# Four moves in the order of work of a two-layer linear-attention and MLP kernel

## The chip, the cores and the metric

The kernel runs on one core of one Trainium2 chip, in one launch. The metric is the device time of that core in microseconds, from several runs of the same program. Engine names are those of the profile: PE is TensorE's matmul (PEld its weight load), DVE is VectorE, ACT is ScalarE, POOL is GpSimd, SP is SyncE, which here issues all DMAs.

## The reference

Two layers, each an attention part A and an MLP part B with residuals, on x of 2048 rows by 640 columns in float32. Layernorm has no weights.

```python
x = x + A(layernorm(x)); x = x + B(layernorm(x))      # twice, same weights

def A(x):                       # 32 heads of 20 columns
    q, k, v = split(x @ wqkv)
    pq, pk = q @ w_phi, k @ w_phi                      # per head, 20 x 20
    phi_q = concat(softmax(pq), softmax(-pq))          # 40 features
    phi_k = concat(softmax(pk), softmax(-pk))
    kv, z = phi_k^T v, sum_s phi_k                     # sums over all rows
    return ((phi_q kv) / (phi_q z + 1e-6)) @ wo

def B(x):                       # 640 -> 1536 -> 640
    h = x @ w1 + b1
    return (h * tanh(softplus(h))) @ w2
```

## The kernel before, in words

Every large product is made of three matmuls of float32r parts: each operand is split into a high part (a copy on ACT, `fold_high`, `Transposed.high`, L376, L290) and a low part (a subtraction, `fold_low` L294, `Transposed.lower` L384, `make_parts` L172), and `project_half` (L446, matmul at L451) multiplies high by high, high by low and low by high. The rows are taken in 8 blocks of 256, each of two tiles of 128.

*Layer by layer.* For each layer `attend_first` (L501) makes features of keys and queries, stores the queries' features transposed to DRAM (`e_d`, L564) and sums phi_k^T v over all rows into one PSUM tile, `kva` (matmuls at L546; the profile has 128 records for two tiles, 2048 in all). `attend_second` (L815) loads the queries' features again (`load`, L769, DMAs at L778 and L796), multiplies by the finished sums (`average`, L825, matmuls at L839), divides, transposes and multiplies by wo (`Rows.half`, L866). `dense` (L949) is the MLP: matmuls at L963 and L1014.

*Blocks of `attend_first`.* The loop at L685 takes for every block the six projections in `order`: in blocks 2 to 6 `k0 k1 v0 v1 q0 q1` (tile 0 and tile 1 of keys, values, queries). Each is a generator. `next(g)` starts one (its matmuls and the copy out of PSUM); `advance()` (L524) gives every pending generator, newest first, one further step. In `features` (L462) the steps are: subtract the per-head maximum and minimum (L477 to L480, one subtraction on POOL or DVE), one exponential on ACT (L483), the sums and their reciprocal and the scaling (L488 to L491; the scaling mostly on POOL). A yield between two of them puts the next step one projection later. `held(i)` (L515) says how many further projections a key tile waits before its sums at L546. The first step, L467, is a POOL memset of the query or key tile. Query tiles have two buffers, so the third query tile (block 1, tile 0) uses that of the first, whose four stores (L564) must have landed.

*The next block's rows.* While block b is projected, block b+1 is prepared: at n = 0 its x is loaded and its mean and variance are computed on DVE and POOL (`fetch_normed`, L504), at n = 2 the rows are normalized on ACT (`normed`, L401, activation at L409), and at n = 3, 4, 5 `nxt.step()` transposes them on PE (L367) and splits them. In layer two the rows come normalized and transposed from DRAM (`load_turned`, L425) and are only split, their low parts on POOL.

*What sets the order.* The kernel is written in one block whose instructions a planner orders by a simulated timeline: on each engine it takes, of the instructions that are ready in its simulation, the one written first. Three things bind it. `act` (L129) ties every activation that goes through it behind the one written before; in the profile all of these have its line, L135. `tc.issue_after(x)` ties instructions behind `x` where both are on one engine. In `written()` (L121, the start of layer one) and in `attend_second` from L877 (PE and SP alone) the order is the written one. On the chip every engine runs its instructions in the order that was planned.

*Blocks of `attend_second`.* L903: an odd block first averages the next two blocks of queries (four groups, 44 records each in the profile), then the two tiles of the block are multiplied by wo in halves, each added to x (L869). SP gets, in written order: the x of block b+1 (L914; its buffer must have been stored), in odd blocks the features of blocks b+3 and b+4 (`phi`, L899), at the end of each block the store of the new x (L937), and then `fetches[b + 1]()` (L940): the raw rows of the MLP weights (L164; 768 KB for a row block of w1, two or three loads of 320 KB for w2) that `makes[b + 1]()` (L938) splits on ACT and POOL at the end of the block after. `fetches[0]` stands ahead of the loop (L888).

*Value tiles.* `v_halves(apart)` (L142) gives one tile of the tag `v` (two buffers) or, with `apart`, two half tiles of the tag `ol` (six buffers), each filled by activations of its own. A value tile and the key tile's features (`big`, five buffers) live until the sums at L546 have read them.

Of the kernel before, what the change touches and what calls it, by code (L numbers as in the profile page):

```python
# [44 lines left out]
def kernel(  # L45
# [416 lines left out]
    def features(ps, e, pool_sub, scale=nc.gpsimd, late=False, after_low=False):  # L462
# [22 lines left out]
        if late:  # L485
            yield
# [14 lines left out]
    def attend_first(layer, x_src, first):  # L501
# [13 lines left out]
        def held(i):  # L515

            b, t = divmod(i, BT)
            if layer and b == 1:
                return (3, 2)[t]
            if not layer and b < 2:  # L520
                return ((3, 1), (4, 1))[b][t]
            return int(t == 0 and b < NB - 1)
# [8 lines left out]
        def keys(xts, i, v):  # L531
            e = big_tile()
            yield from features(project(xts, i % BT, kv_ws, 0, w=QC), e, False,
                                nc.vector if i == NT - 1 else nc.gpsimd, layer and i // BT == 1,
                                not layer and i // BT == 1)
            yield
            for _ in range(held(i)):
                yield
            opens = not summed[0]
            summed[0] = True  # L540
            for r in range(9):
                for j in range(4):
                    h = 3 * (4 * (r // 3) + j) + r % 3
                    if h < H:
                        c, g = divmod(h, H // 2)
                        nc.tensor.matmul(kva[32 * j:32 * j + DH + 1, 40 * r:40 * r + 40],  # L546
                                         v[1][c][:, (DH + 1) * g:(DH + 1) * (g + 1)], e[:, 40 * h:40 * h + 40],
                                         start=(opens and r == 0), stop=(i == NT - 1), skip_group_check=True)

        def queries(xts, i, ps=None):  # L550
            e = query_tile(i)
            yield from features(project(xts, i % BT, q_ws, 0, w=QC) if ps is None else ps, e, not layer or i != BT,
# [132 lines left out]
        for b in range(NB):  # L685
# [10 lines left out]
            vs = [v_halves(b == 2 or (b == 0 and not layer)) for _ in range(BT)]  # L696
# [4 lines left out]
            for n, (kind, t) in enumerate(order):  # L701
# [6 lines left out]
                if b == 0 and n == (1 if layer else 3):  # L708
                    kva = one_tile()
                    nc.vector.memset(kva[:, :360], 0.0)  # L710
# [4 lines left out]
                if b + 1 < NB:  # L715
                    if n == 0 and (b or layer):
                        xt = fetch_normed(b + 1)
                    elif n == 2:
# [15 lines left out]
                else:  # L734
                    next(g)
                    if layer and b == 0 and n == 0:
                        turn()
                    advance()
# [76 lines left out]
    def attend_second(x_src, x_dst, acc, fetches, makes, fetch_next, begin_next):  # L815
# [61 lines left out]
        with tc.manual_schedule(engines={mybir.EngineType.PE, mybir.EngineType.SP}):  # L877
# [25 lines left out]
            for b in range(NB):  # L903
# [11 lines left out]
                if b % 2:  # L915
                    phi(b + 3)
# [22 lines left out]
                if b + 1 < NB:  # L939
# [248 lines left out]
```

## Time and profile before

| what | before |
|---|---|
| median of 3 runs | 1351.21 us (1350.4 to 1353.28) |
| the profiled execution's own time | 1352.93 us |
| its span, first to last instruction | 1351.1 us |
| granted TensorE clock, mean | 1.000 |
| PE busy | 99%, 13056 matmuls |
| DVE, ACT, POOL busy | 77%, 43%, 36% |
| DMA | 174.24 MB, mean 129 GB/s over the span |
| layer one: `attend_first`, `attend_second`, `dense` | to about 245, 351 and 685 us |
| layer two: the same | to about 905, 1010 us and the end |

The profile is of one execution. PE's busy time says that matmuls were in flight, not that they followed one another as closely as they can: their ends are modelled, so the steps between their starts are to be read beside it. A wait names the instruction or transfer whose semaphore came last; "issue" is a wait that nothing in the profile ends. The time of the profiled execution is 1.8 us more than its span.

### The profile page before, as it was taken

The numbers are of one execution on the slowest core, as the hardware profiler recorded it, in microseconds if no ns is written. First come the engines' busy times: TensorE is split into PE (matmuls) and PEld (weight loads), VectorE is DVE, ScalarE is ACT, GpSimd is POOL, SyncE is SP. The second block draws the span as 40 slices with busy tenths as digits, with TensorE's granted clock in tenths as the row PEclk, the third lists the DMA queues.
The fourth block names the chain that finished last, engine by engine and source line by source line (L and its number), as shares of the span: only waits on it lengthen the run. The fifth ranks groups of instructions, "written<-read, shape, count | busy, mean of one in ns | idle before, by whom it ended". The sixth has DMA issues, their size and how long they took to land.

```text
span 1351.1 us, 31372 instructions
## 1 busy us (share of the span) xinstructions
PE 1343.4 (99%) x13056; PEld 1334.2 (99%) x13056; DVE 1043.1 (77%) x1741; ACT 575.3 (43%) x978; POOL 484.1 (36%) x479
## 2 busy tenths in 40 slices
PE   9999999999999999999999999999999999999998
PEld 9999999999999999999999999999999999999998
DVE  6698898876687877778769788789759776677775
ACT  5343444222454554445443334332236444444443
POOL 3266654334322222222226655634351211111112
PEclk9999999999999999999999999999999999999999
DMA  9545445698714442234474544548974231233200
GB/s 329 174 102 121 98 99 108 169 286 271 216 29 91 118 118 72 61 104 114 122 239 109 124 90 90 98 99 255 291 253 117 79 75 37 85 98 98 78 21 21
DMA packets 353359, 174.24 MB, mean 129 GB/s; under 512 B 288193, under 2 KB 324785, under 8 KB 353217
## 3 DMA queue, kind: packets, MB, share of 16 engines
q1 hardware_dynamic: 353217, 172.25, 47.2%
q8 instruction: 102, 1.67, 0.5%
q14 instruction: 40, 0.33, 0.1%
HBM read 106.34 MB, written 65.86 MB: 127 GB/s over the span
## 4 chain that ended last, share of the span: by engine, by line
PE 93%; DVE 3%; DMA 2%; SPq 1%; POOL 1%; issue 1%; ACT 0%; POOLq 0%; ACTq 0%; DVEq 0%
PE one L963 25%; PE mm L1014 24%; PE mm L451 24%; PE one L451 12%; PE mm L839 3%; PE one L367 2%; PE one L546 2%; PE one L1014 1%; DVE r L488 1%; DVE m L477 1%; DMA e_d<-r 1%; PE one L839 1%; DMA xt<-in_x 1%; DMA wp_d<-r1l 1%; SPq L564 0%
## 5 line engine op out<-in xcount | busy, mean ns | idle before, releaser
L989 POOL TENSOR_TENSOR ol<-big,ol 128x512 fp32r<-128x512 f32 (+1 forms) x98 | 132.0, 1347 | 471.5 <-ACT ol L988 401.8
L1014 PE MATMUL mm<-r2h,ol 128*128 128x320 f32 x1240 | 295.8, 309 | 0.0
L963 PE MATMUL one<-xtl,r1h 128*128 128x256 f32 x960 | 268.4, 280 | 0.0
L963 PE MATMUL one<-xth,r1l 128*128 128x256 f32 x960 | 268.2, 279 | 0.0
L963 PE MATMUL one<-xth,r1h 128*128 128x256 f32 x960 | 266.1, 280 | 0.0
L1014 PEld LDWEIGHTS mm<-r2h,ol 128*128 128x128 f32 x1240 | 212.1, 188 | 0.0
L1014 PE MATMUL mm<-r2l,ol 128*128 128x320 f32 x620 | 190.9, 309 | 0.0
L451 PE MATMUL mm<-r1h,xth 128*128 128x304 f32 (+1 forms) x600 | 184.7, 308 | 0.0
L451 PE MATMUL mm<-r1h,xtl 128*128 128x304 f32 (+1 forms) x600 | 183.9, 307 | 0.3 <-POOL xtl L384 0.3
L451 PE MATMUL mm<-r1l,xth 128*128 128x304 f32 (+1 forms) x600 | 184.0, 307 | 0.0
L963 PEld LDWEIGHTS one<-xth,r1l 128*128 128x128 f32 x960 | 180.5, 188 | 0.0
L963 PEld LDWEIGHTS one<-xtl,r1h 128*128 128x128 f32 x960 | 180.4, 188 | 0.0
L963 PEld LDWEIGHTS one<-xth,r1h 128*128 128x128 f32 x960 | 179.8, 188 | 0.0
L978 DVE TENSOR_SCALAR big<-big 128x512 f32<-128x512 f32 (+1 forms) x98 | 55.6, 567 | 120.7 <-ACT big L976 116.3
L976 ACT ACTIVATE big<-one,b1s 128x256 f32<-128x256 f32 x192 | 81.0, 468 | 102.5 <-PE one L963 102.2
L491 POOL TENSOR_TENSOR r<-r,r 128x1280 f32<-128x1280 f32 x32 | 77.8, 2432 | 115.9 <-DVE r L489 105.7
L988 ACT ACTIVATE ol<-big 128x512 fp32r<-128x512 f32 (+1 forms) x98 | 60.7, 620 | 136.3 <-DVE big L987 136.2
L1014 PEld LDWEIGHTS mm<-r2l,ol 128*128 128x128 f32 x620 | 116.5, 188 | 0.0
L980 ACT ACTIVATE big<-big,two 128x512 f32<-128x512 f32 (+1 forms) x98 | 70.1, 715 | 105.6 <-DVE big L979 105.5
L451 PEld LDWEIGHTS mm<-r1h,xth 128*128 128x128 f32 x600 | 112.8, 188 | 0.8
L451 PEld LDWEIGHTS mm<-r1h,xtl 128*128 128x128 f32 x600 | 112.9, 188 | 0.5 <-POOL xtl L384 0.5
L451 PEld LDWEIGHTS mm<-r1l,xth 128*128 128x128 f32 x600 | 112.8, 188 | 0.1
(179 smaller groups left out, 3136.8 us busy)
## 6 DMA issues: line engine op xcount, KB each, us to landing
e_d<-r SPq DMA_DIRECT2D x128, 160.0 KB, 4.0
big<-e_d SPq DMA_DIRECT2D x30, 640.0 KB, 7.7
x_d<-xt SPq DMA_DIRECT2D x23, 640.0 KB, 5.9
xt<-x_d SPq DMA_DIRECT2D x22, 640.0 KB, 4.2
n_d<-xn SPq DMA_DIRECT2D x168, 80.0 KB, 2.2
xt<-in_x SPq DMA_DIRECT2D x16, 640.0 KB, 4.6
xn<-x_d SPq DMA_DIRECT2D x28, 320.0 KB, 4.5
v<-n_d SPq DMA_DIRECT2D x30, 256.0 KB, 3.1
```

Of the source, the lines that this page charges most:

```text
L367: nc.tensor.transpose(ps[:, c, t * P:(t + 1) * P], self.rows[t][:, (c0 + c) * P:(c0 + c + 1) * P], ident)
L451: last_product[0] = nc.tensor.matmul(ps[:, :w], a[:, sl], r, start=(k == 0 and n == 0), stop=(k == KD - 1 and n == 2)).ins
L491: ins = scale.tensor_tensor(eg, eg, r.unsqueeze(2).to_broadcast([P, 2 * H, DH]), op=ALU.mult).ins
L546: nc.tensor.matmul(kva[32 * j:32 * j + DH + 1, 40 * r:40 * r + 40], v[1][c][:, (DH + 1) * g:(DH + 1) * (g + 1)], e[:, 40 * h:40 * h + 40], ...
L839: nc.tensor.matmul(po[c][64 * q:64 * q + 64, GW * j:GW * j + w], phs[g][:n, s0:s0 + 64], kvb[:n, g, :w], start=True, stop=True)
L963: nc.tensor.matmul(ph[:, j, :], l, r, start=(n == 0), stop=(n == 3 * KD - 1))
L976: exps[0] = nc.scalar.activation(part(ta, 0)[:, j - js.start], ph[:, j, :], AF.Exp, bias=b1s[:, 2 * pr + j:2 * pr + j + 1]).ins
L978: nc.vector.tensor_scalar_min(e, e, E_CAP)
L980: nc.scalar.activation(r, n, AF.Ln, bias=two)
L988: nc.scalar.activation(ah[:, js], n, AF.Copy)
L989: nc.gpsimd.tensor_tensor(al[:, js], n, ah[:, js].bitcast(F32), op=ALU.subtract)
L1014: ins = nc.tensor.matmul(pys[t][c][:, :HC], (ah, ah, al)[n][:, j, t * P:(t + 1) * P], w, start=(f == 0 and n == 0), stop=(f == KF - 1 and ...
```

## The change

- `features`: `late` becomes a number of extra yields ahead of the sums. The first query tile of layer one (`i == 0`) gets one, so that its sum, reciprocal, scaling and transpose stand one projection later; in `b == 0` this is behind `last_fold[0]`, the low parts of the folded key weights. In layer two the two key tiles of block 1 get 2 and 1 instead of 1 and 1.
- `held`: in layer one, blocks 2 to 5, key tiles are held 3 and 2 projections instead of 1 and 0, so both tiles' sums stand after the next block's third projection (its first value tile) instead of after its first. In layer two, block 1, both are held 2 instead of 3 and 2.
- `v_halves`: in layer one, blocks 0, 2, 4 and 6 take half tiles, instead of 0 and 2.
- `kva`'s memset in layer one stands behind the last low part of the folded weights on DVE.
- Block 2's rows (layer one, while block 1 is projected) are normalized after the start of the second projection and ahead of its `advance()`, instead of ahead of the third.
- `attend_second`: the raw weights for odd blocks are loaded within their own block, behind the averages and the load of the next x and ahead of `phi`, instead of at the end of the block before. Those for even blocks stay.

```diff
--- before.py
+++ after.py
@@ -459,7 +459,7 @@
     def query_tile(i):
         return r2_wide(10 + i % 2, F32).rearrange("p s d -> p (s d)")
 
-    def features(ps, e, pool_sub, scale=nc.gpsimd, late=False, after_low=False):
+    def features(ps, e, pool_sub, scale=nc.gpsimd, late=0, after_low=False):
 
         eg = e.rearrange("p (g d) -> p g d", d=DH)
         eh = e.rearrange("p (h s d) -> p s h d", s=2, d=DH)
@@ -482,7 +482,7 @@
         yield
         act(e, e, AF.Exp)
         yield
-        if late:
+        for _ in range(late):
             yield
         r = work.tile([P, 2 * H], F32, tag="r", name="r", bufs=2)
         nc.vector.tensor_reduce(r, eg, axis=AX.X, op=ALU.add)
@@ -516,9 +516,11 @@
 
             b, t = divmod(i, BT)
             if layer and b == 1:
-                return (3, 2)[t]
+                return 2
             if not layer and b < 2:
                 return ((3, 1), (4, 1))[b][t]
+            if not layer and b < NB - 2:
+                return (3, 2)[t]
             return int(t == 0 and b < NB - 1)
 
         def advance():
@@ -531,7 +533,7 @@
         def keys(xts, i, v):
             e = big_tile()
             yield from features(project(xts, i % BT, kv_ws, 0, w=QC), e, False,
-                                nc.vector if i == NT - 1 else nc.gpsimd, layer and i // BT == 1,
+                                nc.vector if i == NT - 1 else nc.gpsimd, (BT + 2 - i) * (layer and i // BT == 1),
                                 not layer and i // BT == 1)
             yield
             for _ in range(held(i)):
@@ -549,7 +551,7 @@
 
         def queries(xts, i, ps=None):
             e = query_tile(i)
-            yield from features(project(xts, i % BT, q_ws, 0, w=QC) if ps is None else ps, e, not layer or i != BT,
+            yield from features(project(xts, i % BT, q_ws, 0, w=QC) if ps is None else ps, e, not layer or i != BT, late=int(not layer and not i),
                                 after_low=not layer and i // BT == 1)
 
             b, t = divmod(i, BT)
@@ -693,7 +695,7 @@
                 order = ("v0", "k0", "q0", "v1", "k1", "q1")
             elif b == NB - 1:
                 order = ("k0", "k1", "v0", "v1", "q0")
-            vs = [v_halves(b == 2 or (b == 0 and not layer)) for _ in range(BT)]
+            vs = [v_halves(b == 2 or (not layer and b % 2 == 0)) for _ in range(BT)]
             if 2 <= b < 2 + KD and not layer:
                 with tc.issue_after(last_act[0]):
                     o_ws.append(next(o_gen))
@@ -707,7 +709,8 @@
                         advance()
                 if b == 0 and n == (1 if layer else 3):
                     kva = one_tile()
-                    nc.vector.memset(kva[:, :360], 0.0)
+                    with (nullcontext() if layer else tc.issue_after(last_fold[0])):
+                        nc.vector.memset(kva[:, :360], 0.0)
                 if b == NB - 1 and n == 3:
                     loaded = {0: load(0)}
                     loaded[1] = load_groups(1, 0) + load_rest(1)
@@ -715,7 +718,7 @@
                 if b + 1 < NB:
                     if n == 0 and (b or layer):
                         xt = fetch_normed(b + 1)
-                    elif n == 2:
+                    elif n == 2 and (layer or b != 1):
                         nxt = xt if layer else normed(b + 1, xt, not b)
                     elif n > 2:
                         nxt.step()
@@ -735,6 +738,8 @@
                     next(g)
                     if layer and b == 0 and n == 0:
                         turn()
+                    if b == 1 and n == 1 and not layer:
+                        nxt = normed(2, xt)
                     advance()
                 pending.append(g)
             if b == 1:
@@ -913,6 +918,7 @@
                 if 0 < b < NB - 1:
                     xs[b + 1] = fetch(x_src, b + 1)
                 if b % 2:
+                    fetches[b]()
                     phi(b + 3)
                     phi(b + 4)
                 if b == NB - 3:
@@ -936,7 +942,7 @@
                 xt = xs.pop(b)
                 nc.sync.dma_start(row_block(x_dst, b), xt)
                 makes[b]()
-                if b + 1 < NB:
+                if b % 2 and b + 1 < NB:
                     fetches[b + 1]()
                 tail()
                 if b < NB - 1:
```

## The prediction

> **What bounds the kernel now.** I read the page first: the span, the busy time of each engine, and the chain that ended last.
>
> ```profile
> span 1351.1 us, 31372 instructions
> ...
> PE 1343.4 (99%) x13056; PEld 1334.2 (99%) x13056; DVE 1043.1 (77%) x1741; ACT 575.3 (43%) x978; POOL 484.1 (36%) x479
> ...
> PE 93%; DVE 3%; DMA 2%; SPq 1%; POOL 1%; issue 1%; ACT 0%; POOLq 0%; ACTq 0%; DVEq 0%
> ```
>
> TensorE (PE) is busy for 1343.4 of 1351.1 us, and the change takes no matmul away. Only the time in which PE stands still, or changes from one kind of matmul to another, can be won. So the next view is the list of PE's waits, which is whole here.
>
> ```profile
> PE one L451 <- issue: 1.6, 1, 1.6
> PE one L92 <- POOL ident masks.py:199: 1.3, 1, 1.3
> PE one L367 <- ACT xn L135: 1.0, 1, 1.0
> PE mm L451 <- POOL xtl L384: 0.3, 1, 0.3
> ```
>
> Of the four waits the second is the start and stays. The other three are one place each, and each lies where the change works. These idle times count from a modelled end of the matmul before; what the end can win is the step between starts, which I read from PE's timeline. The most that the change can win is thus a few microseconds, a fifth to a third of a percent.
>
> **Part 1: rows of block 2, and the first query's sum.** PE's timeline, columns start and duration:
>
> ```profile
> 60.32 0.31 PE L451 MATMUL mm<-r1h,xth 128*128 128x320 f32 x1
> 60.47 0.31 PE L451 MATMUL mm<-r1l,xth 128*128 128x320 f32 x1
> 61.80 0.33 PE L367 MATMUL one<-ident,xn 128*128 128x128 f32 x1 [1.02 <-ACT xn L135]
> ```
>
> The second step is 1.33 us, where matmuls of this shape start 0.15 apart: 1.2 us lost, on the transposes of block 2's normalized rows. The chain of waits says what came before:
>
> ```profile
> 52.77 1.20 POOL r L478
> ...
> 54.82 0.19 DVE mv L342 x2
> ```
>
> ACT and POOL in the same stretch, from their timelines:
>
> ```profile
> 56.40 1.13 POOL L352 TENSOR_SCALAR stats<-mv,stats 128x1 f32<-128x1 f32 x2
> 59.67 1.27 ACT L135 ACTIVATE big<-big 128x1280 f32<-128x1280 f32 x1 [2.97 <-DVE big L480]
> 60.84 1.72 ACT L135 ACTIVATE xn<-xt,stats 128x640 f32<-128x640 f32 x2
> ```
>
> The statistics are there at 57.53 (56.40 + 1.13), yet the two normalizations run at 60.84, because every activation of this stretch is held in the order in which it is written, and an exponential that waits for DVE until 59.67 stands ahead. The change writes the normalizations ahead of that step's `advance()`, so ahead of this exponential. They could then run from 57.55 to 59.27 (1.72 for both), in ACT's idle 2.97 us, and the exponential still starts at 59.67: nothing is pushed. The tiles are ready 1.2 us before PE now asks for them at 60.6. If PE is given the transposes at once, before the next projection, it comes at about 59.0 (eleven steps of 0.15 earlier) and waits 0.3. I take 1.2 won; bounds 0.9 and 1.2 as long as the statistics come no later.
>
> The same part holds back the first query's sum by one step:
>
> ```profile
> 34.64 1.50 DVE L561 STREAM_TRANSPOSE r<-r 128x1280 f32<-128x1280 f32 x1
> 44.57 1.66 DVE L340 BATCH_NORM_STATS2 bn<-xt 128x6 f32<-128x320 f32 x4
> 43.30 6.47 SPq L564 DMA_DIRECT2D e_d<-r  x4
> 53.99 0.82 DVE L480 TENSOR_TENSOR r<-m,r 128x640 f32<-128x640 f32 x1 [7.77 <-POOL r L478]
> 52.61 0.16 POOL L467 MEMSET r<- 128x32 f32 x1 [17.97 <-DMA e_d<-r]
> ```
>
> The sum (L488) leaves the middle of the fold lows and goes behind them; the low parts come that much sooner, but PE waits for none of them, so that is worth nothing. The query's transpose (34.64) moves a step later too. Its four stores are issued at 43.30, long after it, because SP's queue has the weight spills in front: the transpose may slip by 7.2 us (43.30 - 34.64 - 1.50) before a store is later. The row at 52.61 is what hangs on these stores: POOL clears the next query tile in the same buffer and holds the second query's subtraction (52.77 in the chain), for which DVE sits idle 7.77 us, with the statistics queued behind (54.82). The order of POOL is a planner's; if the later store makes it put the subtraction ahead of the memset, the whole chain starts up to 7.8 us sooner and the 0.3 goes as well. The memset of the sums' accumulator moves on DVE behind the lows; the sums that need it come a block later.
>
> **Part 2: sums of blocks 2 to 5.** The key-value sums (L546) move two steps later. Today, between projections:
>
> ```profile
> 108.30 1.48 PE L546 MATMUL one<-big,ol 128*21 128x40 f32 x128
> 109.70 0.41 PE L451 MATMUL mm<-r1h,xth 128*128 128x304 f32 x1
> 109.95 0.30 PE L451 MATMUL mm<-r1l,xth 128*128 128x304 f32 x1
> ```
>
> After the sums, the first step of a projection takes 0.25 us (109.70 to 109.95) instead of 0.14. Right ahead of transposes the two changes of kind fall together and 0.1 us is saved, four times: 0.4 at best, 0 if a projection still stands between. I take 0.2. The value tiles of blocks 4 and 6 become halves: two more activations for each of four tiles, none as long as the 1.27 us row above, under an ACT that is 43% busy; cost nothing, and at most some 10 us of ACT, spread over four tiles, if PE ever waited for ACT there. The tiles that live longer (four of five `big` buffers) still fit.
>
> **Part 3: layer two, block 1.** The sum of the first key tile goes one step later, its matmuls stay (two yields late and two held, instead of one and three). POOL and PE:
>
> ```profile
> 740.06 2.36 POOL L491 TENSOR_TENSOR big<-big,r 128x1280 f32<-128x1280 f32 x1
> 742.38 1.32 POOL L384 TENSOR_TENSOR xtl<-xn,xth 128x256 fp32r<-128x256 f32 x1
> ...
> 743.05 0.30 PE L451 MATMUL mm<-r1h,xth 128*128 128x304 f32 x1
> 743.19 0.30 PE L451 MATMUL mm<-r1l,xth 128*128 128x304 f32 x1
> 743.75 0.41 PE L451 MATMUL mm<-r1h,xtl 128*128 128x304 f32 x1 [0.26 <-POOL xtl L384]
> ```
>
> The 2.36 us scaling stands ahead of the last low part, which PE awaits: a step of 0.56 instead of 0.14. With the scaling behind, the low part starts at about 740.1. Won: 0.4. What is late next is the scaled key tile, by 1.3 us, whose matmuls come much later.
>
> **Part 4: raw weights behind averages.** PE's largest wait:
>
> ```profile
> 318.00 1.36 PE L839 MATMUL mm<-kvb,big 120*64 120x63 f32 x40
> ...
> 319.39 0.41 PE L451 MATMUL one<-r2h,xth 128*128 128x320 f32 x1
> 321.45 0.42 PE L451 MATMUL one<-r2l,xth 128*128 128x320 f32 x1 [1.65 <-issue]
> ```
>
> 2.06 us between starts: 1.9 lost, released by nothing that the profile shows. The DMA view of 315.1 to 319.1 gives the first line below, that of 319.1 to 320.1 the second; the third is the page's, for the span:
>
> ```profile
> q1 hardware_dynamic: 207, 0.80, 92.3%
> ...
> q8 instruction: 1, 0.02, 5.5%
> ...
> q8 instruction: 102, 1.67, 0.5%
> ```
>
> 102 packets of instructions, 16 KB each, feed the 13056 matmuls and their weight loads: 256 instructions a packet. In the four microseconds before the stall none came, with the engines 92.3% busy on SP's transfers; then one came and PE went on. I read it as PE out of instructions: 128 of the averages' small matmuls use up a packet in 4.4 us (1.36 us for 40). SP at that place:
>
> ```profile
> 314.52 0.33 SPq L498 DMA_DIRECT2D xt<-in_x  x1
> 314.95 0.38 SPq L937 DMA_DIRECT2D x_d<-xt  x1
> 315.38 2.85 SPq L164 DMA_DIRECT2D raw<-in_w  x3
> ```
>
> The change takes the three raw loads from here to behind the next block's x. But x and its store (640 KB each) stay, and the earlier odd block's raw load, 768 KB, moves in front of the e_d loads that end just before. Bounds: 1.9 won if the packet comes in time, 0 if it still meets a full queue. I take 1.2, nearer to a win because PE also comes by at another moment of that queue. The transfers are the same in number and size; those now later are raw weights, which ACT and POOL split at the end of the block, with half a block to land.
>
> [...]
>
> **The sum.** 1.2 + 0.2 + 0.4 + 1.2 = 3.0 us. The profiled execution took 1352.93 for its span of 1351.1, so it would take 1349.9. It lies 1.7 above the median of the runs, 1351.21; I carry the difference over, so 1348.2.
>
> **Rivals.** *The packet stays late* (or its stall, seen in one execution, is not in the median run): the parts but the fourth give 1.8, so 1349.4. For it: the queue is as full without the raws. Against: only one of 102 packets stalls PE, so a small shift is enough.
>
> *The first query's stores come late.* If DVE takes the transpose only after the statistics' row at 44.57, it ends at 47.7. With as long from the first issue to POOL's release as now (43.30 to 52.61), POOL goes on at 57.0, not 52.6: 4.4 us late. The statistics come 4.9 after that release today (57.53) and both normalizations 1.72 later: 63.7, where PE asks at 59.0 to 60.6. It waits 3.1 to 4.7 instead of 1.2. DVE, which is 4.4 us behind, has no room to catch up (busy us of PE, PEld, DVE, ACT, POOL):
>
> ```profile
> 90.00:100.00 10.00, 10.00 (x192) 9.73 (x191) 10.00 (x12) 4.69 (x10) 5.50 (x4) 1.00 0.43 122
> ```
>
> So part 1 may cost 4.4 in place of winning 1.2: 4.4 - 0.2 - 0.4 - 1.2 = 2.6 slower, 1353.8. It begins to count once the transpose slips by more than 7.2 us, and turns the whole change into a loss when PE's wait grows by the 1.8 that the other parts win: with the release 2.7 us late if PE asks at 59.0 (wait: late + 0.3, less 1.2), 4.3 if at 60.6. For it: DVE runs in one planned order, and its gap before 53.99 is where a late transpose would fit. Against: there are 1.78 us idle on DVE before 38.50, when the scaled query is about ready, and a planner sees the transpose early.
>
> ```profile
> 38.50 1.55 DVE L477 TENSOR_REDUCE m<-big 128x32 f32<-128x640 f32 x2 [1.78 <-ACT big L135]
> ```
>
> **How the numbers follow.** The forecast, 3.0 us faster, has 0.50; the late packet 0.30; the late stores 0.20. A measurement of this kernel tells about 0.2% from no change, 2.7 us, so the bounds are 1348.5 and 1353.9. The forecast alone runs from 1347.3 (all bounds won: 1.2 + 0.4 + 0.4 + 1.9 = 3.9) to 1349.0: I put 0.42 of its 0.50 under 1348.5. Of the late packet 0.05 is under it, 0.23 within, 0.02 above 1353.9; of the late stores 0.13 above and 0.07 within. That makes faster 0.47, same 0.38, slower 0.15. The range is 1346.8 (3.9 won and half a microsecond of the runs' scatter) to 1353.0: it leaves out some 0.05 below and 0.15 above.
>
> **What would show it.** Part 1: no wait of PE on the normalized rows; the normalizations ahead of the exponential on ACT; POOL's subtraction ahead of the memset, or the memset released no later than 52.6. Part 2: transposes right behind the sums on PE in four blocks. Part 3: no wait on the low part near 743. Part 4: no step over 0.3 us behind the averages in either layer, an instruction packet ahead of the time at which PE needs it. Wrong would be: the same or another wait on "issue" among the averages; a wait for an e_d load there, since the raw loads now stand ahead of these; PE waits for DVE in blocks 2 to 5; a planner's order that changes more than the moved pieces.

## The result, and the profile after

The kernel after takes 1349.44 us (median of 22 runs, 1348.68 to 1351.06), the kernel before 1351.28 us on the same chip (22 runs, 1349.73 to 1355.54). The medians lie 1.84 us apart. The ratio is 0.9983, with a 95% interval of 0.9977 to 0.9989, which is 1.5 to 3.1 us: the gain is clear of no change at all, but under the 2.7 us (0.2%) that the prediction set as its bound of "faster". So the outcome that it thought likeliest (faster, 0.47) did not come, and "same" (0.38) did. The time lies 1.24 us above the 1348.2 forecast, inside the range. The profiled executions lie further apart: 1349.24 against 1352.93 us, 3.69 us. This difference between the pair and the medians is the main thing to explain.

The page of the kernel after: its span, the engines and the chain that ended last.

```profile
span 1347.4 us, 31386 instructions
...
PE 1342.2 (100%) x13056; PEld 1333.4 (99%) x13056; DVE 1045.7 (78%) x1741; ACT 577.3 (43%) x986; POOL 480.2 (36%) x479
...
PE 100%; issue 0%; ACT 0%; DVE 0%; POOL 0%; POOLq 0%
```

In the chain DVE is down from 3% to 0%, and DMA and SP have left it. PE's waits, all of them:

```profile
PE one L92 <- POOL ident masks.py:199: 1.3, 1, 1.3
PE mm L451 <- DVE r1l L334: 0.4, 1, 0.4
PE one L274 <- issue: 0.2, 1, 0.2
```

The waits on the normalized rows, on the instruction packet and on layer two's low part are gone. A wait of 0.4 us on a folded low part is new, and one of 0.2 us ahead of the first projection. To add this up I took the start of the n-th matmul of `project_half` in both traces; the growth of the difference shows where time comes from (some of the expectations below call this the ledger). There are four stretches in which anything moves: the first to the 561st matmul (13 to 107 us, part 1), the 561st to the 1301st (to 224 us, part 2), the 1701st to the 1801st (around 320 us, part 4) and the 2251st to the 2331st (around 740 us, part 3).

| stretch | before | after | won |
|---|---|---|---|
| part 1: block 1 to 2, layer one | 93.61 | 92.75 | 0.86 |
| part 2: blocks 3 to 6 | 117.56 | 117.38 | 0.18 |
| part 4: averages of block 5 | 24.23 | 22.31 | 1.92 |
| part 3: block 1, layer two | 11.72 | 11.20 | 0.52 |

Together 3.48, which is the whole distance of the pair but 0.2 at the ends of the span. The rows behind each line, first POOL and ACT around block 2's rows:

```profile
45.19 1.28 POOL L478 TENSOR_TENSOR r<-r,m 128x640 f32<-128x640 f32 x1 [6.04 <-DVE m L477]
51.88 0.16 POOL L467 MEMSET r<- 128x32 f32 x1 [5.42 <-DMA e_d<-r]
...
54.09 0.50 POOL L352 TENSOR_SCALAR stats<-mv,stats 128x1 f32<-128x1 f32 x2
```

```profile
55.97 1.72 ACT L135 ACTIVATE xn<-xt,stats 128x640 f32<-128x640 f32 x2
57.59 1.26 ACT L135 ACTIVATE big<-big 128x1280 f32<-128x1280 f32 x1
```

POOL now subtracts at 45.19, ahead of the memset that waits for the stores, where before it subtracted at 52.77, behind it. The statistics are ready at 54.59 and not at 57.53, and the normalizations run ahead of the exponential.

The new wait, from DVE's and PE's timelines:

```profile
31.83 1.62 DVE L334 TENSOR_TENSOR r1l<-mm,r1h 128x570 fp32r<-128x570 f32 x4 [1.45 <-ACT r1h L135]
```

```profile
32.15 0.27 PE L318 MATMUL one<-ol,r 64*64 64x38 f32 x4
32.83 0.38 PE L451 MATMUL mm<-r1h,xth 128*128 128x304 f32 x1 [0.42 <-DVE r1l L334]
```

With the sum (L488) gone from between the low parts, DVE stands idle for 1.45 us, because the next low part waits for ACT's high part. The planner also put block 1's first four transposes, which PE ran at 32.32 before, behind the first key matmuls. PE comes to these 0.4 us too early. But that order is not needed for such a wait: the kernel with only layer two changed (below), which runs the transposes at 32.32 as before, waits 0.4 us on the same low part.

The sums of block 2 on PE, with transposes right behind, as in blocks 3 to 5:

```profile
116.05 1.48 PE L548 MATMUL one<-big,ol 128*21 128x40 f32 x128
117.45 0.66 PE L367 MATMUL one<-ident,xn 128*128 128x128 f32 x4
117.86 0.39 PE L451 MATMUL mm<-r1h,xth 128*128 128x320 f32 x1
118.09 0.31 PE L451 MATMUL mm<-r1l,xth 128*128 128x320 f32 x1
```

Only one return to the projection's matmuls costs its 0.09 us (117.86 to 118.09 against 0.14 to 0.15) where there were two. Against that the first step among the transposes takes 0.16 us where 0.11 is usual, so some 0.05 is saved a block. The averages of block 5 on PE, and the DMA queues of 310 to 316 us (packets, MB, share of 16 engines):

```profile
318.17 0.27 PE L844 MATMUL mm<-kvb,ol 80*64 80x42 f32 x4
318.37 0.41 PE L451 MATMUL one<-r2h,xth 128*128 128x320 f32 x1
318.62 0.31 PE L451 MATMUL one<-r2l,xth 128*128 128x320 f32 x1
```

```profile
q1 hardware_dynamic: 1321, 2.17, 100.7%
q8 instruction: 1, 0.02, 1.1%
```

The step behind the averages is 0.25 us where it was 2.06. An instruction packet came before 316, although SP's transfers kept the engines full. Last, POOL in layer two: the low parts stand ahead of the scaling, and PE waits for neither.

```profile
735.55 2.00 POOL L384 TENSOR_TENSOR xtl<-xn,xth 128x512 fp32r<-128x512 f32 x2
737.51 2.37 POOL L491 TENSOR_TENSOR big<-big,r 128x1280 f32<-128x1280 f32 x1
```

### The profile page after: what moved, and what is told of

Read it like the earlier page. It is cut to its first block, busy times and chain, and to the rows that moved or that the text cites. A ratio compares the mean times of both kernels' runs of the same rounds, so it can differ in the third digit from the quotient of the medians.

```text
span 1347.4 us, 31386 instructions
## 1 busy us (share of the span) xinstructions
PE 1342.2 (100%) x13056; PEld 1333.4 (99%) x13056; DVE 1045.7 (78%) x1741; ACT 577.3 (43%) x986; POOL 480.2 (36%) x479
## 4 chain that ended last, share of the span: by engine, by line
PE 100%; issue 0%; ACT 0%; DVE 0%; POOL 0%; POOLq 0%
PE mm L451 28%; PE one L969 25%; PE mm L1020 24%; PE one L451 13%; PE mm L844 3%; PE one L367 2%; PE one L548 2%; PE one L1020 1%; PE one L844 1%; PE one L92 0%; PE mm L274 0%; PE one L274 0%; PE mm L318 0%; ACT r1h L135 0%; PE one L811 0%
## 5 line engine op out<-in xcount | busy, mean ns | idle before, releaser
L451 PE MATMUL mm<-r1h,xth 128*128 128x304 f32 (+1 forms) x600 | 184.6, 308 | 0.4 <-DVE r1l L334 0.4
L451 PE MATMUL mm<-r1l,xth 128*128 128x304 f32 (+1 forms) x600 | 183.7, 306 | 0.0
L451 PE MATMUL mm<-r1h,xtl 128*128 128x304 f32 (+1 forms) x600 | 183.5, 306 | 0.0
L451 PEld LDWEIGHTS mm<-r1h,xth 128*128 128x128 f32 x600 | 112.8, 188 | 0.9 <-ACT r1h L135 0.5
L451 PEld LDWEIGHTS mm<-r1l,xth 128*128 128x128 f32 x600 | 112.8, 188 | 0.1
L451 PEld LDWEIGHTS mm<-r1h,xtl 128*128 128x128 f32 x600 | 112.8, 188 | 0.0
```

What stands on the lines that cost most here:

```text
L451: last_product[0] = nc.tensor.matmul(ps[:, :w], a[:, sl], r, start=(k == 0 and n == 0), stop=(k == KD - 1 and n == 2)).ins
```

## The experiments

Each median stands beside runs of the kernel before on the same chip; their medians were 1350.97 us for the first four kernels below, 1351.11 for the rows, the first query's sum, the sums of blocks 2 to 5 and layer two alone, 1351.52 for both edits of part 1, the change without the sum and the transposes first, and 1351.41 for the change without the rows. Each kernel was profiled once. The stretches are those of the table above.

**Half a packet and a whole packet.** Tiny matmuls (20 by 20) behind the warm-up shift the instruction stream of the kernel before by 128 and by 256 instructions, and change no other instruction.

```diff
+    for _ in range(32):
+        nc.tensor.matmul(warm[:20, :20], ident[:, :20], ident[:, :20], start=True, stop=True)
```

The second has `range(64)`.

> The kernel before with 32 tiny matmuls (20 by 20, 64 records, 128 instructions with their weight loads) behind the warm-up, so that the limits of the 256-instruction packets lie half a packet earlier in all that follows; DMAs are the same. Theory (PE out of instructions): the step of 2.06 us behind the averages of block 5 in layer one is gone, since no request falls into these averages with less than 8 us to spare; instead the requests fall early into the averages of block 5 of layer two (about 975) and perhaps of block 1 (about 924), where a transfer late by over 1.9 us stalls PE: a wait on issue of 1 to 3 us there is likely. Rival (the wait is for a buffer, a semaphore or the operand of that line): it stays where it is, at the second matmul behind the averages of block 5 in layer one, and none comes elsewhere.

> As half_packet with 64 tiny matmuls, 256 instructions: a whole packet, so the limits lie where they lay before, and the time is the same but for up to 1 us at the start. Theory: when a wait on issue is seen, it is behind the averages of block 5 in layer one, of about 1 to 2.5 us, and none in layer two; it may be missing in one execution, since it hangs on how full the DMA queue is at that moment. Rival (tiny matmuls move the work against the DMAs by their own time): half_packet and whole_packet look alike.

Half a packet: 1352.81 us, ratio 1.0011 [1.0003, 1.002]; no wait on issue anywhere, part 4's stretch 22.31. The wait that was called likely in layer two did not come. A whole packet: 1353.01, ratio 1.0017 [1.0009, 1.0026]; the wait is back:

```profile
320.73 0.41 PE L453 MATMUL one<-r2h,xth 128*128 128x320 f32 x1
321.70 0.41 PE L453 MATMUL one<-r2l,xth 128*128 128x320 f32 x1 [0.55 <-issue]
```

Counted from 0 over PE's whole stream (matmuls, weight loads and the few instructions of its sequencer between them), the weight load of the matmul that stalls is number 7873 in the kernel before and 8129, that is 7873 + 256, here. Five kernels that follow stall at number 7873 too, while the matmul standing there differs (L451 or one of the averages). So the wait belongs to a place in the instruction stream, which comes again one packet on, and not to the data. The medians of both are no price of a packet: the tiny matmuls delay the first projection (14.87 and 15.79 us instead of 13.19).

**The raw weights alone, and the change without them.** Part 4 on the kernel before; and the kernel after with part 4 undone (both lines the other way round).

```diff
+                    fetches[b]()
                     phi(b + 3)
...
-                if b + 1 < NB:
+                if b % 2 and b + 1 < NB:
                     fetches[b + 1]()
```

> The kernel before with the raw weights of odd blocks behind the averages, and nothing else changed. Theory: PE keeps the waits of 1.2 us (block 2's rows) and 0.4 us (layer two, block 1); the wait on issue is gone, 1.9 us less than the profile of before; the runs over 1352.5 us, 8 of 22 before, are gone, while the lowest runs stay near 1350, so the median falls by 0.3 to 1 us only. Rival (the move wins the 1.9 us in every run): all runs near 1349.

> The changed kernel with the raw weights loaded where they were before. Theory: lowest runs near 1349, as the changed kernel; some runs 2 to 4 us above them, with a wait on issue among the averages of block 5 if the profile is one of these; median 0 to 1 us over the changed kernel's 1349.4. Rival (the raw move gives all of the gain): median near 1351.

Raw weights alone: 1350.57 us (11 runs, none above 1351.9), ratio 0.9999 [0.999, 1.0007]; no wait on issue, part 4's stretch 22.31. One expectation failed here, and it is the one to learn from: the waits on block 2's rows and on layer two's low part are not there either (part 1's stretch 92.52, part 3's 11.51), although PE, DVE, ACT and POOL run the same instructions in the same order as in the kernel before. So these two waits come and go without the edits that were made against them. Without the raw weights' move: 1350.21 (12 runs, up to 1355.56), ratio 0.9995 [0.9983, 1.0007], stretch 23.19 and

```profile
PE mm L844 <- issue: 0.6, 1, 0.6
```

This part takes the wait away, but the median hardly shows it: its effect seems to be in the upper runs. Over 1352.5 us lie 30 of 131 runs of the kernel before (all comparisons together), 19 of 69 of the six kernels tried without part 4 and without tiny matmuls, and none of 63 of the five with it. (Of the six, both edits of part 1 have none of 11, so not every kernel without part 4 shows it.)

**The rows alone.** Only block 2's normalization earlier, on the kernel before.

```diff
-                    elif n == 2:
+                    elif n == 2 and (layer or b != 1):
...
+                    if b == 1 and n == 1 and not layer:
+                        nxt = normed(2, xt)
                     advance()
```

> The kernel before with block 2's rows normalized ahead of the waiting exponential, nothing else. Theory (the wait on these rows is set by when the first query's stores land, 52.5 us in the profile of before and 51.1 in that of raw_alone, and by the exponential ahead of them): the normalizations run about 1.4 us earlier against the landing, PE's wait on them is 0 to 0.3 us at any landing up to 52.6. Steps of 0.56 us in layer two, block 1, stay. Median 0 to 0.8 us under before, since only some executions of before have the wait. Rival (order on ACT does not matter, only the landing does): the wait of about 1.2 us is there when the stores land at 52.5.

1352.88 us, ratio 1.0009 [1.0, 1.0017]; 0 to 0.8 us under the kernel before had been expected, and the median is 1.8 above. PE's wait at 61 us is gone, but PE and DVE show another one 16 us later:

```profile
77.07 0.30 PE L451 MATMUL mm<-r1l,xth 128*128 128x304 f32 x1
78.40 0.41 PE L451 MATMUL mm<-r1h,xtl 128*128 128x304 f32 x1 [1.02 <-DVE xtl L384]
```

```profile
76.59 1.43 DVE L488 TENSOR_REDUCE r<-r 128x64 f32<-128x1280 f32 x1
77.94 0.41 DVE L384 TENSOR_TENSOR xtl<-one,xth 128x256 fp32r<-128x256 f32 x1
```

The kernel after at the same place:

```profile
72.93 0.40 DVE L384 TENSOR_TENSOR xtl<-one,xth 128x256 fp32r<-128x256 f32 x1
```

Block 2's last low part ends at 78.35, in the kernel after at 73.33. DVE was late too: POOL still holds the second query's subtraction back behind its memset,

```profile
52.27 0.16 POOL L467 MEMSET r<- 128x32 f32 x1 [16.95 <-DMA e_d<-r]
52.35 1.28 POOL L478 TENSOR_TENSOR r<-r,m 128x640 f32<-128x640 f32 x1
```

DVE waits for POOL and is behind, and so block 2 gets its rows sooner but its low parts no sooner. Part 1's stretch takes 93.77.

**The first query's sum alone.** The other half of part 1: sum and memset behind the low parts, on the kernel before (with `late` a number, as in the change).

```diff
-            yield from features(project(xts, i % BT, q_ws, 0, w=QC) if ps is None else ps, e, not layer or i != BT,
+            yield from features(project(xts, i % BT, q_ws, 0, w=QC) if ps is None else ps, e, not layer or i != BT, late=int(not layer and not i),
...
-                    nc.vector.memset(kva[:, :360], 0.0)
+                    with (nullcontext() if layer else tc.issue_after(last_fold[0])):
+                        nc.vector.memset(kva[:, :360], 0.0)
```

> The kernel before with the first query's sum and the accumulator's memset behind the fold lows, nothing else. Theory: POOL does the second query's subtraction at about 45, ahead of the memset that waits for the stores, DVE's idle 7.8 us before 54 is gone, and PE does not wait for block 2's rows; but the planner puts the transposes of block 1 behind the first key matmuls, so PE waits 0.4 us for a low part near 32 and the step from the folds is 0.64 us. Net: 0.4 us slower where before had no wait on the rows, 0.8 faster where it had: median within 0.5 us of before. Rival (the 0.4 us comes from another part): no wait near 32 here.

1351.28 us, ratio 0.9999 [0.999, 1.0008]. PE waits neither at 61 nor at 77, and the 0.4 on a folded low part is there: the stretch takes 92.77, as with the whole change. The median does not show it. The profiled execution, 1354.72 us, also had the longest packet wait of all:

```profile
318.47 0.41 PE L451 MATMUL one<-r2h,xth 128*128 128x320 f32 x1
321.45 0.64 PE L451 MATMUL one<-r2l,xth 128*128 128x320 f32 x1 [2.56 <-issue]
```

**Both edits of part 1**, on the kernel before (the two diffs above).

> The kernel before with both edits of part 1 (block 2's rows normalized ahead of the second projection's steps; the first query's sum and the accumulator's memset behind the low parts), and nothing else. Theory: the two belong together. The rows' edit alone turned the wait at 61 into a wait of 1.0 on a low part near 77, since DVE was late; the sum's edit releases POOL sooner and so brings DVE forward, which takes that second wait away. So there are no waits of PE over 0.3 on xn or xtl between 55 and 80 us; the ledger of matmul starts against before stands at about -0.8 (1.2 won, 0.4 lost near 32) from 80 us to 315 us; the wait on issue of 0.6 to 2.6 behind layer one's averages stays, at PE instruction 7873; the median is 0.4 to 1.0 under that of before. Rival (the two edits do not help each other, the gain at 61 is a draw of the execution): a wait of 0.7 to 1.3 on xn or xtl stands between 55 and 80 us, and the median is within 0.3 of before or above it.

1350.62 us, ratio 0.9988 [0.9979, 0.9997]; stretch 92.75. There is no wait on block 2's rows or low parts, and the packet's wait stays, as the theory has it:

```profile
PE one L451 <- issue: 1.7, 1, 1.7
...
PE mm L451 <- DVE r1l L334: 0.4, 1, 0.4
```

**The change without the first query's sum, and without the rows.** The two diffs undone one at a time in the kernel after.

> The kernel after, with the first query's sum and the accumulator's memset put back to where they stood before. Theory (the sum's edit costs 0.4 at 32 and pays by starting POOL's subtraction ahead of the memset): the ledger against after is -0.4 at 36 us, and between 55 and 80 us PE waits 0.7 to 1.3 for the normalized rows or for a low part, so that it is +0.4 to +0.9 behind; median 0.3 to 1.0 above after's 1349.4. Rival (the sum's edit only costs): no wait over 0.3 between 55 and 80 us, median 0.4 under after.

> The kernel after, with the normalization of block 2's rows put back behind the second projection's steps. Theory now (the sum's edit alone ends both the wait at 61 and the one at 77, the rows' edit adds nothing): no wait of PE over 0.3 on xn or xtl between 55 and 80 us; from the first projection matmul to the 561st there are 92.7 to 92.8 us, as in all five kernels with the sum's edit (92.73 to 92.77); median within 0.3 of after's 1349.4. Rival (the prediction's own step, the rows' edit is what wins 1.2): a wait of 0.9 to 1.2 on xn at 61 comes back, the stretch takes 93.6 to 94.0, median about 1350.6.

Without the sum: 1351.16 us, ratio 0.9995 [0.9986, 1.0004], stretch 94.36, with waits on low parts of both kinds (and one of 0.3 us on ACT near 109 us, which falls in part 2's stretch):

```profile
PE mm L451 <- DVE xtl L384: 0.8, 1, 0.8
PE mm L451 <- DVE r1l L334: 0.5, 1, 0.5
```

Without the rows: 1349.43 us, ratio 0.9983 [0.9974, 0.9992], the same as the whole change; stretch 92.77. So the rows' edit, to which the prediction gave 1.2 us, is worth nothing once the sum is moved, and what part 1 wins, the sum's edit wins. (That edit has two halves, the query's sum and the accumulator's memset, which were not run apart.) The theory that the sum's edit only costs fell; so did "the loss of 0.4 comes from the sum", since the wait on a folded low part is also there with the sum put back. (This execution without the rows had a wait of 1.1 us on a low part at 995 us, which no other shows; its cause stays open.)

**The sums of blocks 2 to 5 alone** (`held` and the half tiles, on the kernel before).

```diff
+            if not layer and b < NB - 2:
+                return (3, 2)[t]
...
-            vs = [v_halves(b == 2 or (b == 0 and not layer)) for _ in range(BT)]
+            vs = [v_halves(b == 2 or (not layer and b % 2 == 0)) for _ in range(BT)]
```

> The kernel before with the sums of blocks 2 to 5 two steps later and the half tiles, nothing else. Theory: 0.05 us a block, 0.2 us in all, by steps between matmul starts; median within 0.5 us of before, not to be told from it. The sums stand right ahead of the transposes in four blocks. Rival (longer-lived tiles cost something): waits of PE on ACT or DVE in blocks 3 to 6.

1352.28 us, ratio 1.0005 [0.9995, 1.0015]; the median is 1.2 us above the kernel before, where at most 0.5 had been expected, but no change at all lies inside the interval. Its stretch takes 117.35: 0.2 won, as in the kernel after, and PE waits for neither ACT nor DVE in it. The packet wait of this execution,

```profile
317.39 0.26 PE L841 MATMUL mm<-kvb,ol 80*64 80x42 f32 x3
319.28 0.25 PE L841 MATMUL mm<-kvb,ol 80*64 80x42 f32 x1 [1.62 <-issue]
```

and what followed it (last section) cost 3.4 us in part 4's stretch (25.73), far more than the 0.2.

**Layer two, block 1, alone** (part 3 on the kernel before, with `late` a number here too).

```diff
-                return (3, 2)[t]
+                return 2
...
-                                nc.vector if i == NT - 1 else nc.gpsimd, layer and i // BT == 1,
+                                nc.vector if i == NT - 1 else nc.gpsimd, (BT + 2 - i) * (layer and i // BT == 1),
```

> The kernel before with the first key tile's sum of layer two, block 1, one step later, nothing else. Theory: POOL does the last low part of block 1 ahead of the scaling; the step of 0.56 us near 743 (0.3 us wait on a low part) is gone: 0.4 us, seen in the profile, hardly in the median. Rival (POOL's later scaling then delays a later low part or the sums): a wait on POOL later in layer two, blocks 1 to 3, of as much.

1350.82 us, ratio 0.9996 [0.9987, 1.0004]; its stretch takes 11.20. In layer one, where nothing is changed and PE, DVE, ACT and POOL keep the order of the kernel before, this execution waits 0.4 us on a folded low part near 33 us and 0.3 on block 2's rows, and part 1's stretch takes 93.40.

**Transposes first.** The kernel after, with block 1's first key matmuls tied behind the four transposes of that step, as PE ran them before the change.

```diff
-                    nc.tensor.transpose(ps[:, c, t * P:(t + 1) * P],
+                    last_turn[0] = nc.tensor.transpose(ps[:, c, t * P:(t + 1) * P],
...
-                    with tc.issue_after(last_product[0]):
+                    with tc.issue_after((last_turn if n == 3 else last_product)[0]):
```

> The kernel after, with the first key tile of the step at 32 us tied behind the four transposes of that step, so that PE takes them ahead of the first key matmul as it did before the change. Theory (the loss of 0.40 near 32 comes from the planner's new place for four transposes): the wait on r1l there is gone, steps of 0.3 or less; ledger against after -0.4 from 36 us to the end; median 0.2 to 0.6 under after, about 1349.0, the fastest of all kernels here. Rival (PE waits for the folded low part either way, because the low parts themselves are late): a wait of 0.3 or more on r1l or a step over 0.5 stays between 31 and 37 us, and the median is within 0.2 of after's 1349.4.

1349.12 us (8 runs, 1348.59 to 1349.86), ratio 0.9976 [0.9965, 0.9988]. It is the lowest median of all, but its interval overlaps that of the kernel after, which was measured beside other runs of before, so the two are not told apart. The profile speaks for the rival, though the wait is earlier than it said: PE's wait moved to 31.04 us, among the folds, of which the planner has also changed places:

```profile
PE mm L318 <- DVE r1l L334: 0.3, 1, 0.3
```

and part 1's stretch takes 92.73 against 92.75. In this execution block 1's rows landed late (DVE's statistics start 12.8 us after the first projection, 12.0 in the kernel after), so whether the order helps when they land sooner is open.

## Why the prediction was right, and where it was wrong

The four stretches in all fourteen profiled executions, split by whether the kernel has the edit:

| stretch (edit) | without the edit | with the edit |
|---|---|---|
| part 1 (first query's sum) | 92.31 to 94.36, mean of eight 93.21 | 92.73 to 92.77 (six) |
| part 2 (sums later) | 117.56 to 117.62 (eight) | 117.35 to 117.38 (five; 117.94 without the sum) |
| part 4 (raw weights) | 22.31 to 26.50, mean of nine 23.96 | 22.31 (five) |
| part 3 (layer two, block 1) | 11.41 to 12.47, mean of eight 11.67 | 11.20 (six) |

This table is the answer. Part 2 is a fixed saving. The other three remove waits whose length is a draw, that is, changes from one execution to the next: without the edit the stretch wanders, with it the number stands still. That this is the execution and not the kernel is shown for part 1 by the six kernels with neither of its edits: on PE (but for the tiny matmuls), DVE, ACT and POOL they run the same order up to about 106 us, and yet take 92.31 to 93.61. For part 4 the kernel with layer two alone shows it, which is the kernel before throughout layer one (22.31 and 24.23), and for part 3 the raw weights alone, whose four engines keep the order throughout (11.51 and 11.72). A single execution's wait is not the wait of the median run.

*Part 1, 1.2 (bounds 0.9 to 1.2).* In the profiled pair 0.86: the 1.2 came, less the new 0.4. The step that failed is which of the two edits wins it. The text gave the 1.2 to the normalizations ahead of the exponential and said of the fold lows that their earlier time "is worth nothing"; the runs show that the sum's edit wins all (POOL subtracts 7.6 us sooner, the "up to 7.8" named in passing), and that the rows' edit alone only moves PE's wait to DVE's low part. Nor did the low parts come much sooner: 31.83 for 31.93 us, since they wait for ACT. And the size was one draw: the six kernels with neither edit take 92.31 to 93.61, mean 92.93, so over executions part 1 wins about 0.2 (92.93 - 92.75), and in three of the six it would have won nothing.

*Part 2, 0.2.* Right: 0.18 to 0.2, by the mechanism named.

*Part 3, 0.4.* Right: 0.52 in the pair, 0.47 in the mean, and at least 0.2 in every kernel (11.41 - 11.20).

*Part 4, 1.2 (0 to 1.9).* The mechanism was right: PE lacked instructions (the stall moves from number 7873 to 8129 with one packet more). In the pair it won 1.92, the upper bound; over executions 1.65 (23.96 - 22.31), seven of the nine without the edit stall there and none of the five with it. Of the 102 packets of the kernel before this one alone stalls PE (one wait on issue, 1.6 us). What makes it late is finer than "a full queue", which the kernel after has too (100.7% from 310 to 316 us). When a packet is asked for stands in no row, but the traces bound it: in all fourteen the transfer of packet n (counted from 0) begins when PE stands at instruction 157 + 256 n or behind it, never more than 3 ahead, and some 40 of the 102 begin within ten instructions of it (41 in the kernel before, 45 in the kernel after). I take that as the asking; for the packet that is late it is instruction 7581, 292 ahead of the stall. In the seven kernels that stall, PE goes on 2.2 to 2.4 us after the transfer begins, and its loss is the time from the asking to that beginning less 2.0 to 2.4 us. Against SP's issue of the next x and of the store of the last one the asking gives:

| kernel | asked for | x, store issued | packet landing begins | part 4's stretch |
|---|---|---|---|---|
| before | 315.06 | 314.52, 314.95 | 319.18 | 24.23 |
| the sum alone | 314.14 | 313.13, 313.84 | 319.01 | 26.50 |
| without the raws | 313.75 | 312.36, 313.51 | 316.51 | 23.19 |
| layer two alone | 314.89 | 314.86, 315.28 | 316.07 | 22.31 |
| raw weights alone | 313.61 | 314.64, 315.07 | 314.76 | 22.31 |
| after | 313.92 | 315.11, 315.53 | 315.42 | 22.31 |

Asked for behind the store, the packet takes 2.8 to 4.9 us to begin; ahead of it, 0.8 to 1.5. The other three kernels that stall at number 7873, the whole packet and the other three with part 4 fall the same way. With half a packet the request goes out at 310.61, behind the earlier block's store (307.79) and raw loads; it takes 4.0 us too, but PE needs the packet only 4.1 us after the transfer begins. So the part of the text that failed is the cure: it is not the three raw loads that leave the packet's way (with layer two alone they stand where they were, and the packet is in time). The order of x, store and packet is turned round. In SP's timeline of the kernel after the raw loads come only 6 us later:

```profile
315.11 0.33 SPq L498 DMA_DIRECT2D xt<-in_x  x1
315.53 1.35 SPq L943 DMA_DIRECT2D x_d<-xt  x1
...
321.90 1.37 SPq L164 DMA_DIRECT2D raw<-in_w  x3
```

The x waits for its buffer, about 7.6 us after the earlier store in both kernels, and that store stands 8.1 us ahead of the request before (306.97) and 6.5 after (307.45). Why SP comes later there against PE, probably since the odd block's 768 KB now stand in front of its queue, is argued and not shown.

*The sum.* 3.0 for the pair, measured 3.69. For the median 3.0 was too much, and the step that failed is the last one: "it lies 1.7 above the median; I carry the difference over". The profiled execution lay 1.7 high because it carried waits that the change removes: 25 of the 131 runs of the kernel before took as long. The forecast of that execution, 1352.93 - 3.0 = 1349.9, should not have been lowered again: the profiled execution after took 1349.24 us, the median run 1349.44. Adding the means of the table (0.2 + 0.2 + 1.65 + 0.47) gives 2.5; leaving out half a packet, which moves the packet by itself, changes the terms (0.1, 0.2, 1.85, 0.35) and not the sum. The means of the runs, 1351.87 and 1349.61, lie 2.26 apart, the medians 1.84. Of the parts tried on the kernel before, only the two edits of part 1 together are faster by runs alone (0.9988 [0.9979, 0.9997]); that the four parts add up to the gain rests on the stretches. The upper end of the forecast, 1349.0, was also too low for its own bounds: with each part at its least (0.9, 0, 0.4, 0) 1.3 us are won, which is 1349.9, and the 1349.44 that came lies between.

*The rivals.* The late packet's 1349.4 is the time that came, but not for its reason: the packet comes in time. Its second clause, that the stall is not in the median run, is nearer: the stall varies from nothing to 4.2 us of the stretch, and in the median it may count for less than in the pair. The late stores did not come: the transpose runs at 39.18 us, ahead of the statistics, and the memset is released at 51.88 instead of 52.61. What the list of doubts had right is "a planner's order that changes more than the moved pieces": four transposes on PE that nothing in the change names.

## What to carry to other kernels

Where the profiled execution lies above the median of the runs, ask first whether the waits that a change removes are the reason: then they are worth less than the profile shows, and the gap must not be carried over. To price a wait that depends on a DMA's landing, profile several kernels that leave it alone and compare the same stretch of matmuls; one that wanders is a draw (here part 4, 22.31 to 26.50 us without the edit), one that stands still is a fixed cost (part 2, 117.56 to 117.62). Where kernels run the same order of instructions in a stretch, their differences there are draws and no effect of an edit (92.31 to 93.61 us in six kernels). When a wait has two late engines behind it, undo each edit by itself: bringing the visible one forward can leave the wait where the other one is late (1.02 us at 78.40 with the rows alone).

## What the runs showed of the hardware that was not expected

In two executions the late packet cost more than its wait: in the windows behind it PE's granted clock is below 1. In the execution with the sum alone, by windows of 2 us (busy us of PE, PEld, DVE, ACT and POOL, each with its count, then granted clock, DMA share, GB/s):

```profile
320.00:322.00 2.00, 0.55 (x2) 0.56 (x3) 0.72 (x2) 0.00 (x0) 0.20 (x1) 0.77 0.54 211
322.00:324.00 2.00, 2.00 (x9) 2.00 (x8) 0.00 (x0) 0.00 (x0) 0.00 (x0) 0.50 0.98 314
324.00:326.00 2.00, 2.00 (x14) 2.00 (x14) 0.80 (x2) 0.00 (x0) 0.00 (x0) 0.88 0.86 344
```

Its matmuls start 0.27 us apart for nine steps, where 0.147 is usual:

```profile
322.15 0.47 PE L451 MATMUL one<-r2h,xth 128*128 128x320 f32 x1
322.41 0.47 PE L451 MATMUL one<-r2l,xth 128*128 128x320 f32 x1
```

With the step of 2.98 us ahead of it this cost 4.2 us (26.50 - 22.31). The same happened behind a step of 1.85 us in the kernel with part 2 alone (clock 0.58 and 0.57 in two windows), but not behind steps of 2.06 (before) and 2.15 us (both edits of part 1), where every window shows 1.00. The clock that is missing adds up to the same in both kernels: (0.23 + 0.50 + 0.12) x 2 us and (0.42 + 0.43) x 2 us, 1.7 us of full speed each. Why the clock fell behind 1.85 us and not behind 2.15 us is not shown.
